# A padded scratch tile moves TensorE's moving operands by 32 bytes in SBUF

## The chip, the cores and the metric

The kernel runs on one core of one Trainium2 chip. The metric is the device time of one execution in microseconds (us); lower is better. The core has five engines that matter here: TensorE (PE in the profile, its weight loads PEld), VectorE (DVE), ScalarE (ACT), GpSimd (POOL) and SyncE (SP, which issues DMAs). SBUF is the on-chip memory of 128 partitions in which every tile lies; PSUM takes TensorE's results.

## The reference

The input is `x` of 8 batches, 3072 positions and 256 features. It goes through a two-dimensional Fourier transform of which the real part is kept, and each of the 24576 rows then goes through a small network with one hidden layer of 2048.

```python
X = np.fft.fft(np.fft.fft(x, axis=1), axis=2).real      # 8 x 3072 x 256
h = X.reshape(-1, 256) @ w_in                            # 24576 x 2048
g = h * np.tanh(np.log1p(np.exp(h)))                     # Mish
out = g @ w_out                                          # 24576 x 256
```

All of it is float32, and the kernel keeps float32 accuracy in matrix products by splitting each factor into a high and a low part.

## The kernel before

The feature transform is multiplied into `w_in` once at the start, which gives a cosine weight and a sine weight. Each is split in two tiles, `wch` and `wcl`, `wsh` and `wsl`; the output weights are `woh` and `wol`. The position transform uses symmetry: DVE and POOL fold the rows of a batch into the tiles `F0e`, `F0o`, `F1e` and `F1o`, and TensorE multiplies these, as weights, with a table `dft`, as the moving operand (`transform`, L365, plain float32). A matmul here has two operands: the weights are loaded into the array beforehand by a LDWEIGHTS (128 columns), and the moving operand is streamed through column by column.

The results of `transform` are combined and split by `first_chunk`, `other_chunks` and `last_chunk` into the tiles `ph`, `pl`, `qh` and `ql`. A batch has three chunks of 512 columns, a chunk 16 steps of the main loop, and the loop 8 x 3 x 16 = 384 steps. The tile `base` is a scratch tile of these functions: DVE writes a result of `transform` there, and the scaling and splitting instructions read it.

Each step of the main loop does this:

- `mm1` (L695 to L697): six matmuls of 512 columns, moving `ph`, `pl`, `qh`, `ql` (type float32r), weights a slice of `wch`, `wcl`, `wsh`, `wsl`.
- `make_h` (L704 to L706): DVE takes the two PSUM results into a ring of nine tiles, `hring`; ACT then applies Mish (L810).
- `split`, eight steps later: ACT casts to `gh` (L714), POOL subtracts to `gl` (L715).
- `mm2`, ten steps later: twelve matmuls of 512 columns (L725), moving `gh` (eight) and `gl` (four), weights slices of `woh` and `wol`.

So a step has 18 such matmuls, each with its own LDWEIGHTS, and the order on each engine is written out by hand. Between steps stand the fold of the next batch, the `transform` matmuls, and once, in the last batch, `single_h` and `single_out`, which compute one position left out by the symmetry. In `single_out` (L783 to L785) the roles are turned round: `woh` and `wol` are moving, 256 columns at a time, and the weights are 8 columns of `endgh` or `endgl`, which lie in the places of `F1e` and `F1o`.

Where a tile lies is set by the order of the pools. The built program puts each tile at the next multiple of 32 bytes in the partition, in the order constants, fold tiles (`fold`, where `base` stands after the `F` tiles and ahead of `full0`, `full1` and `spare`), the split tiles (`ql`, `pl`, `ph`, `qh`), `p0b`, `ot`, and the tiles `gl` and `gh`. In bytes past a multiple of 64, the built program has:

| tile | role in the matmuls | before |
|---|---|---|
| wch, wcl, wsh, wsl, woh, wol | weights in the main loop; woh and wol move in `single_out` | 32 |
| ph, pl, qh, ql, gh, gl | moving, float32r, 512 columns | 0 |
| F0e, F0o, F1e, F1o | weights of `transform` | 32 |
| dft (slices) | moving, float32: 0, 8, 16 or 24 for the even outputs, 16 (`F0`) and 32 (`F1`) for the odd ones | 0 to 32 |
| hring, xring | read and written by DVE, ACT and POOL | 0 |

Past a multiple of 512 all six moving tiles lie at 0, and all slices of the main loop's weights at 288.

Of the kernel before, what the change touches and what calls it, by code (L numbers as in the profile page):

```python
# [10 lines left out]
F32 = mybir.dt.float32  # L11
# [18 lines left out]
NE = 258  # L30
# [182 lines left out]
def fft_moe(ctx, tc, x, col_d, mids_d, w_in, w_out, cs_d, dft_d, ysel_d, out, single_d):  # L213
# [4 lines left out]
    def pool(name, bufs=1, **kw):  # L218
        return ctx.enter_context(tc.tile_pool(name=name, bufs=bufs, **kw))
# [3 lines left out]
    fp = pool("fold")  # L223
# [7 lines left out]
    def ps(tag):  # L231
        return psab.tile([128, 512], F32, tag=tag, name=tag)
# [48 lines left out]
    def fold_part(b, c, y, i, par):  # L281
        return folds[b][c, y][:, par if COSINE[y][i] else 1 - par, i]
# [71 lines left out]
    def const(c, par, sine):  # L354
        if par == 0:
            o = NE * sine
            return dft[:, c, o:o + NE]
        o = 2 * NE + 256 * sine
        return dft[:, c, o:o + 256]

    def transform(dst, lhs, par, sine, mid_lhs=None, halves=(0, 1), **kw):

        last = 1 if mid_lhs is None else 2
        for c in halves:
            T.matmul(dst, lhs(c), const(c, par, sine), **{"start": c == 0, "stop": c == last, **kw})  # L365
        if mid_lhs is not None and 1 in halves:

            n = dst.shape[-1]
            T.matmul(dst, mid_lhs, alt[0:1, None, :].to_broadcast([1, n // 2, 2]), **{**kw, "start": False, "stop": True})
# [3 lines left out]
    def new_chunk(ch):  # L373
        q = {}
        for n in ("ph", "pl", "qh", "ql"):
            q[n] = pqp.tile([128, 512], F32R, tag=n, name=n)
        chunks[ch] = q

    def split_to(hi, lo, src, eng):
        A.copy(hi, src)  # L380
        eng.tensor_tensor(lo, src, hi, op=ALU.subtract)  # L381

    def add_mid(dst, src, i, b):

        pairs = (y[:, :NE].rearrange("p (a s) -> p a s", s=2) for y in (dst, src))
        dst, src = pairs
        V.scalar_tensor_tensor(dst, alt[:, None, :].to_broadcast([128, NE // 2, 2]), midc[:, i, b:b + 1], src,
                               op0=ALU.mult, op1=ALU.add)

    def first_chunk(b, par, part=(0, 1, 2)):  # L390

        ch = 3 * b
        st = folds[b]
        n = NE if par == 0 else 256
        sl = slice(256 * par, 256 * par + 256)
        if 0 in part:
            st["ps", par] = ps("pa"), ps("pb")
        pa, pb = st["ps", par]
        halves = [c for c in (0, 1) if c in part]
        transform(pa[:, :n], lambda c: fold_part(b, c, "e", 0, par), par, 0, None, halves)  # L400
        transform(pb[:, :n], lambda c: fold_part(b, c, "o", 0, par), par, 1, None, halves)
        if b == 0 and par == 1 and 1 in part:

            T.matmul(pb[:, :n], mid0, const(0, 1, 1)[0:1], start=False, stop=True, skip_group_check=True)
        if 2 in part:
            if par == 0:
                new_chunk(ch)
            q = chunks[ch]
            if par == 0:
                base = fp.tile([128, NE], F32, tag="base", name="base")  # L410
                add_mid(base, pa, 0, b)
                pa = base
            split_to(q["ph"][:, sl], q["pl"][:, sl], pa[:, :256], V)
            split_to(q["qh"][:, sl], q["ql"][:, sl], pb[:, :256], V)
            if par == 0:
                V.tensor_copy(ends[:, b:b + 1], pa[:, 256:257])

    def other_chunks(b, par, odd):

        ch = 3 * b + 1  # L420
        if par == 0 and not odd:
            new_chunk(ch)
            for o in range(2):
                full2[o] = fp.tile([128, 512], F32, tag=f"full{o}", name=f"full{o}")
        st = folds[b]
        n = NE if par == 0 else 256
        sl = slice(256 * par, 256 * par + 256)
        pa, pb = ps("pa"), ps("pb")
        y, cos, sin = ("o", 2, 1) if odd else ("e", 1, 2)
        transform(pa[:, :n], lambda c: fold_part(b, c, y, cos, par), par, 0)  # L430
        transform(pb[:, :n], lambda c: fold_part(b, c, y, sin, par), par, 1)

        base = fp.tile([128, NE], F32, tag="base", name="base")
        spare = fp.tile([128, 256], F32, tag="spare", name="spare")
        if par == 0:
            add_mid(base, pa, 1 + odd, b)
        else:
            V.tensor_copy(base[:, :n], pa[:, :n])

        def combine(dst, sg, o):  # L440
            scaled, plain = (base, pb) if odd else (pb, base)
            V.scalar_tensor_tensor(dst, scaled[:, o:o + 256], sg, plain[:, o:o + 256], op0=ALU.mult, op1=ALU.add)

        combine(spare, R3 if odd else -R3, 0)
        q = chunks[ch]
        h, l = ("qh", "ql") if odd else ("ph", "pl")
        split_to(q[h][:, sl], q[l][:, sl], spare, G)
        combine(full2[odd][:, sl], -R3 if odd else R3, 1 if par == 0 else 0)
# [225 lines left out]
    def chunk0(par, part):  # L674
        first_chunk(0, par, (part,))
# [115 lines left out]
    for tau in range(NS + LAG_M):  # L791
# [17 lines left out]
        if tau < NS:  # L809
            A.activation(hring[:, tau % RH], hring[:, tau % RH], AF.Mish)  # L810
            for f in early.pop(tau, []):
                f()
            other_at = OTHER_AT if b else OTHER0_AT
            if r in other_at:
                i = other_at.index(r)
                other_chunks(b, i % 2, i // 2)
            if r in LAST_AT:
                last_chunk(b, LAST_AT.index(r))
            if r == FOLD_AT[b > 0] and b + 1 < NB:
                fold_q = fold_ops(b + 1)  # L820
                pace = sum(cost for cost, _ in fold_q) / (FOLD_AT[2] - r)
                spent = goal = 0.0
            if fold_q:
                goal += pace
                while fold_q and spent + fold_q[0][0] / 2 <= goal + 1e-9 or fold_q and r == FOLD_AT[2]:
                    cost, f = fold_q.pop(0)
                    spent += cost
                    f()
            if b + 1 < NB and r in FIRST_AT:
                first_chunk(b + 1, FIRST_AT.index(r))  # L830
            if tau % NF == P0_AT and tau // NF + 1 < 3 * NB:
                load_p0(tau // NF + 1)
            if b == NB - 1 and r == 20:
                single = single_h()
            if b == NB - 1 and r == 22:
                single_out(single)
# [29 lines left out]
```

## Time and profile before

| | |
|---|---|
| median of 3 runs | 1838.26 us (1837.71 to 1840.17) |
| the profiled execution | 1837.48 us, of which the trace spans 1835.7 us |
| TensorE matmuls (PE) busy | 1773.7 us, 97% of the span |
| TensorE weight loads (PEld) busy | 1410.2 us, 77% |
| DVE, ACT, POOL busy | 1229.0, 903.7, 1236.4 us (67%, 49%, 67%) |
| mean granted TensorE clock | 0.982 of full |

Busy time of matmuls overlaps with that of the next ones, since matmuls are pipelined: one of 512 columns is shown as some 0.40 us long, while the next starts before that time is up. What a matmul costs in a chain of them is read from the distance between starts. The granted clock is given as a share of 2.4 GHz, so 0.50 is 1.2 GHz.

### The profile page before, as it was taken

How to read it: one execution, taken by the hardware profiler on the slowest of the kernel's cores; microseconds unless marked ns; L12 is line 12 of the kernel's file. 1: busy time of each engine (PE TensorE's matmuls, PEld its weight loads, DVE VectorE, ACT ScalarE, POOL GpSimd, SP SyncE). 2: the span in 40 equal slices, each digit the busy share in tenths (PEclk: the TensorE clock that was granted, in tenths of full speed). 3: DMA queues.
4: the chain of work that ended last, by engine and by line, in shares of the span. 5: the costliest groups of instructions: out<-in, count | busy, mean ns of one | idle time of the engine just before them, and what ended most of it. 6: DMA issues, size and time to landing. Idle time of an engine off the chain costs nothing.

```text
span 1835.7 us, 20673 instructions
## 1 busy us (share of the span) xinstructions
PE 1773.7 (97%) x7540; PEld 1410.2 (77%) x7540; DVE 1229.0 (67%) x1609; ACT 903.7 (49%) x980; POOL 1236.4 (67%) x653
## 2 busy tenths in 40 slices
PE   5688999999999999999999999999999999998999
PEld 3366778888888888888888888888888888887887
DVE  7566785677856876577856777568865778553552
ACT  2455454455545555455545555455544555452453
POOL 4368885687756876587756876578765877553556
PEclk8789999999999999999999999999999999998999
DMA  4120200200002000100002000020002000000000
GB/s 170 35 76 29 80 26 4 98 1 30 29 1 98 29 1 29 60 39 29 29 1 98 28 3 29 1 98 29 12 18 97 1 29 30 1 29 1 30 24 23
DMA packets 25016, 67.65 MB, mean 37 GB/s; under 512 B 3027, under 2 KB 3258, under 8 KB 24786
## 3 DMA queue, kind: packets, MB, share of 16 engines
q1 hardware_dynamic: 24354, 64.86, 9.6%
q8 instruction: 59, 0.97, 0.2%
q10 hardware_dynamic: 560, 1.47, 0.2%
q14 instruction: 43, 0.35, 0.1%
HBM read 41.07 MB, written 25.25 MB: 36 GB/s over the span
## 4 chain that ended last, share of the span: by engine, by line
PE 90%; POOL 4%; DVE 2%; issue 2%; ACT 1%; DMA 1%; SPq 0%; DVEq 0%; POOLq 0%
PE acc L725 56%; PE pa L695 5%; PE pa L696 5%; PE pb L695 5%; PE pa L697 5%; PE pb L697 5%; PE pb L696 5%; PE pa L365 2%; PE pb L365 2%; POOL gl L715 1%; ACT gh L714 1%; PE pw L518 1%; POOL xring L504 1%; POOL xring L505 0%; DVE hring L704 0%
## 5 line engine op out<-in xcount | busy, mean ns | idle before, releaser
L715 POOL TENSOR_TENSOR gl<-hring,gh 128x1024 fp32r<-128x1024 f32 x384 | 925.6, 2411 | 515.8 <-ACT gh L714 477.2
L714 ACT CAST gh<-hring 128x1024 fp32r<-128x1024 f32 x384 | 402.8, 1049 | 464.4 <-PE acc L725 464.1
L725 PE MATMUL acc<-gh,woh 128*128 128x512 f32 x1536 | 609.0, 396 | 4.0 <-ACT gh L714 2.2
L725 PE MATMUL acc<-gh,wol 128*128 128x512 f32 x1536 | 607.4, 395 | 0.0
L810 ACT ACTIVATE hring<-hring 128x1024 f32<-128x1024 f32 x384 | 407.3, 1061 | 338.1 <-DVE hring L706 312.9
L704 DVE SCALAR_TENSOR_TENSOR hring<-p0b,wc,pa 128x512 f32<-128x512 f32 x384 | 285.3, 743 | 425.6 <-POOL gl L715 411.8
L725 PE MATMUL acc<-gl,woh 128*128 128x512 f32 x1536 | 433.7, 396 | 2.2 <-POOL gl L715 2.2
L725 PEld LDWEIGHTS acc<-gh,woh 128*128 128x128 f32 x1536 | 288.6, 188 | 76.6 <-ACT gh L714 3.5
L725 PEld LDWEIGHTS acc<-gl,woh 128*128 128x128 f32 x1536 | 288.7, 188 | 73.3 <-POOL gl L715 3.5
L725 PEld LDWEIGHTS acc<-gh,wol 128*128 128x128 f32 x1536 | 289.0, 188 | 69.4 <-POOL wol L537 0.4
L705 DVE TENSOR_TENSOR hring<-hring,pb 128x512 f32<-128x512 f32 x384 | 264.1, 688 | 41.1 <-PE acc L725 0.9
L706 DVE TENSOR_TENSOR hring<-hring,pb 128x512 f32<-128x512 f32 x384 | 263.7, 687 | 13.3
L695 PE MATMUL pa<-ph,wch 128*128 128x512 f32 x384 | 162.8, 424 | 4.0 <-DVE hring L704 4.0
L695 PE MATMUL pb<-qh,wsh 128*128 128x512 f32 x384 | 153.4, 399 | 3.0 <-DVE hring L706 2.6
L696 PE MATMUL pb<-ql,wsh 128*128 128x512 f32 x384 | 152.5, 397 | 0.3 <-POOL ql L381 0.3
L697 PE MATMUL pa<-ph,wcl 128*128 128x512 f32 x384 | 152.6, 398 | 0.0
L696 PE MATMUL pa<-pl,wch 128*128 128x512 f32 x384 | 152.6, 397 | 0.0
L697 PE MATMUL pb<-qh,wsl 128*128 128x512 f32 x384 | 152.3, 396 | 0.0
L695 PEld LDWEIGHTS pb<-qh,wsh 128*128 128x128 f32 x384 | 72.9, 190 | 23.8 <-DVE hring L706 6.0
L695 PEld LDWEIGHTS pa<-ph,wch 128*128 128x128 f32 x384 | 72.6, 189 | 23.3 <-DVE hring L704 4.9
L696 PEld LDWEIGHTS pb<-ql,wsh 128*128 128x128 f32 x384 | 72.6, 189 | 18.0 <-POOL ql L381 0.6
L697 PEld LDWEIGHTS pa<-ph,wcl 128*128 128x128 f32 x384 | 72.6, 189 | 17.7
(192 smaller groups left out, 1343.3 us busy)
## 6 DMA issues: line engine op xcount, KB each, us to landing
xring<-x_dram SPq DMA_DIRECT2D x32, 768.0 KB
out_dram<-ot SPq DMA_DIRECT2D x96, 256.0 KB
p0b<-p_d SPq DMA_DIRECT2D x23, 256.0 KB
xring<-w_out_dram SPq DMA_DIRECT2D x8, 512.0 KB
hring<-w_in_dram SPq DMA_DIRECT2D x4, 512.0 KB
dft<-table_dft_dram ACTq DMA_DIRECT2D x1, 1028.0 KB
winr<-w_in_dram SPq DMA_DIRECT2D x2, 512.0 KB
xring<-w_in_dram SPq DMA_DIRECT2D x2, 512.0 KB
```

What stands on the lines that cost most here:

```text
L365: T.matmul(dst, lhs(c), const(c, par, sine), **{"start": c == 0, "stop": c == last, **kw})
L504: G.tensor_tensor(t, t, vf, op=ALU.add)
L695: T.matmul(dst, wh[:, fs], q[n + "h"], start=True, stop=False)
L696: T.matmul(dst, wh[:, fs], q[n + "l"], start=False, stop=False)
L697: T.matmul(dst, wl[:, fs], q[n + "h"], start=False, stop=True)
L704: V.scalar_tensor_tensor(h[:, 0:512], p0b[ch], wc0[:, f:f + 1], pa, op0=ALU.mult, op1=ALU.add)
L705: V.tensor_tensor(h[:, 512:1024], h[:, 0:512], pb, op=ALU.add)
L706: V.tensor_tensor(h[:, 0:512], h[:, 0:512], pb, op=ALU.subtract)
L714: A.copy(gh, h)
L715: G.tensor_tensor(gl, h, gh, op=ALU.subtract)
L725: T.matmul(acc[i], w[:, f, 128 * d:128 * d + 128], g[:, 512 * t:512 * t + 512], **kw)
L810: A.activation(hring[:, tau % RH], hring[:, tau % RH], AF.Mish)
```

## The change

The scratch tile `base` is allocated 14 float32 longer, 1088 bytes in a partition and not 1032, and is used through a view of its first 258 columns as before. The padding is never read or written.

```diff
             if par == 0:
-                base = fp.tile([128, NE], F32, tag="base", name="base")
+                base = fp.tile([128, NE + 14], F32, tag="base", name="base")[:, :NE]
                 add_mid(base, pa, 0, b)
...
-        base = fp.tile([128, NE], F32, tag="base", name="base")
+        base = fp.tile([128, NE + 14], F32, tag="base", name="base")[:, :NE]
         spare = fp.tile([128, 256], F32, tag="spare", name="spare")
```

No engine's instructions change in number, order or waits. In the built programs the room taken by `base` grows from 1056 to 1088 bytes, and each tile behind it lies 32 bytes further: `full0`, `full1`, `spare`, `ph`, `pl`, `qh`, `ql`, `p0b`, `ot`, `gh`, `gl` go from 0 to 32 past a multiple of 64 (and of 512). All others stay where they were: the weights, `dft`, the `F` tiles, `hring`, `xring`, and `base` itself.

## Rows read from the trace of the kernel before

**Rows 1.** The page: span and busy time of each engine.
```profile
span 1835.7 us, 20673 instructions
PE 1773.7 (97%) x7540; PEld 1410.2 (77%) x7540; DVE 1229.0 (67%) x1609; ACT 903.7 (49%) x980; POOL 1236.4 (67%) x653
```
**Rows 2.** Stretches of the main part: busy us and instructions, clock, DMA share, GB/s.
```profile
core 0: us, PE busy (x) PEld busy (x) DVE busy (x) ACT busy (x) POOL busy (x), PEclk, DMA share, GB/s
500.00:1000.00 500.00, 500.00 (x2155) 404.79 (x2155) 343.18 (x440) 252.90 (x265) 341.18 (x173) 1.00 0.10 38
1000.00:1500.00 500.00, 500.00 (x2152) 404.17 (x2151) 358.36 (x445) 256.34 (x265) 357.16 (x184) 1.00 0.09 32
```
**Rows 3.** Waits, longest in total: us, times, longest.
```profile
POOL gl L715 <- ACT gh L714: 477.2, 271, 16.7
ACT gh L714 <- PE acc L725: 464.1, 357, 11.5
DVE hring L704 <- POOL gl L715: 411.8, 214, 5.0
ACT hring L810 <- DVE hring L706: 312.9, 304, 3.1
```
**Rows 4.** The page: costliest groups of matmuls, with counts.
```profile
L725 PE MATMUL acc<-gh,woh 128*128 128x512 f32 x1536 | 609.0, 396 | 4.0 <-ACT gh L714 2.2
L725 PE MATMUL acc<-gh,wol 128*128 128x512 f32 x1536 | 607.4, 395 | 0.0
...
L725 PE MATMUL acc<-gl,woh 128*128 128x512 f32 x1536 | 433.7, 396 | 2.2 <-POOL gl L715 2.2
...
L695 PE MATMUL pa<-ph,wch 128*128 128x512 f32 x384 | 162.8, 424 | 4.0 <-DVE hring L704 4.0
```
**Rows 5.** Timeline of PE over one step, first and last rows: start us, us.
```profile
800.60 0.40 PE L695 MATMUL pa<-ph,wch 128*128 128x512 f32 x1
800.84 0.40 PE L696 MATMUL pa<-pl,wch 128*128 128x512 f32 x1
...
803.87 1.10 PE L725 MATMUL acc<-gl,woh 128*128 128x512 f32 x4
804.80 0.40 PE L695 MATMUL pa<-ph,wch 128*128 128x512 f32 x1
```
**Rows 6.** Timeline of PE, `transform` of the odd outputs.
```profile
500.29 0.59 PE L365 MATMUL pa<-dft,F0e 128*128 128x256 f32 x2
500.72 0.59 PE L365 MATMUL pa<-dft,F1e 128*128 128x256 f32 x2
501.15 0.59 PE L365 MATMUL pb<-dft,F0o 128*128 128x256 f32 x2
501.58 0.59 PE L365 MATMUL pb<-dft,F1o 128*128 128x256 f32 x2
```
**Rows 7.** Timeline of PE in a stretch of lower clock.
```profile
206.04 0.63 PE L695 MATMUL pa<-ph,wch 128*128 128x512 f32 x1
206.47 0.63 PE L696 MATMUL pa<-pl,wch 128*128 128x512 f32 x1
206.89 0.63 PE L697 MATMUL pa<-ph,wcl 128*128 128x512 f32 x1
```
**Rows 8.** Windows: clock in that stretch and at the end of `single_out`.
```profile
204.20:207.40 3.20, 3.20 (x9) 2.45 (x9) 3.06 (x5) 1.62 (x2) 3.04 (x2) 0.50 0.65 206
...
1697.00:1698.30 1.30, 1.30 (x14) 1.02 (x12) 0.00 (x0) 0.00 (x0) 0.00 (x0) 1.00 0.07 13
```
**Rows 9.** Timeline of PE, last matmuls of `single_out`.
```profile
1697.08 0.28 PE L783 MATMUL pa<-woh,endgh 128*8 128x256 f32 x1
1697.19 0.28 PE L784 MATMUL pa<-wol,endgh 128*8 128x256 f32 x1
...
1698.32 0.28 PE L785 MATMUL pa<-woh,endgl 128*8 128x256 f32 x1
```
**Rows 10.** Weight loads by form: the main loop's, and `single_out`'s: busy us, mean ns.
```profile
L725 PEld LDWEIGHTS acc<-gh,wol 128*128 128x128 f32 x1536 | 289.0, 188 | 69.4 <-POOL wol L537 0.4
...
L365 PEld LDWEIGHTS pb<-dft,F1o 128*128 128x128 f32 x64 | 12.0, 189 | 2.0 <-DVE F1o L319 0.3
...
L784 PEld LDWEIGHTS pa<-wol,endgh 128*8 128x8 f32 x4 | 0.4, 88 | 0.1
```

## The prediction

> **What bounds the kernel now.** I read the page's first part, then the stretches, then the waits. TensorE's matmuls are busy for 1773.7 us of the 1835.7 us span [rows 1], and between 500 and 1500 us without a gap, at a granted clock of 1.00 [rows 2]. The other engines are busy 50 to 72% there, and the waits that they lead, ACT's for TensorE (464.1 us) and through it POOL's and DVE's, end at TensorE's work [rows 3]. So the end of the kernel moves with what one matmul costs from its start to the next one's, and with nothing else as long as POOL and DVE keep their 28 to 32% of slack.
>
> That cost is read from the timeline. A step of the main loop goes from 800.60 to 804.80 us [rows 5] and has 18 matmuls of 512 columns: 4.20 / 18 = 0.2333 us each. There are 3 x 1536 + 6 x 384 = 6912 of them [rows 4], and 6912 x 0.2333 = 1613 us, 88% of the span. One nanosecond on each is 6.9 us, 0.38% of the time.
>
> Now what the 233 ns consist of. The plain float32 matmuls of `transform` start at 500.29 and at 501.58 us with six passes between, 1.29 / 6 = 0.215 us for a pass [rows 6]. Their weight loads are as long as the main loop's, 189 and 188 ns [rows 10]. In the stretch with a granted clock of 0.50 (1.2 GHz) [rows 8], main-loop matmuls start 0.85 / 2 = 0.425 us apart [rows 7], some 213 ns at full speed if the clock were all. So at 2.4 GHz a float32r matmul of 512 columns costs about 18 ns more than the 215 ns of a float32 pass, with the same weight load beside it. At 1.2 GHz the excess is not there. I read it as the moving columns not always coming as fast as the array at 2.4 GHz takes them. It is 18 x 6912 = 124 us in all, and it is the one thing that the place of a moving operand could change.
>
> **The change part by part.** Nothing is added, removed or reordered on any engine. Two kinds of access change place.
>
> First, DVE, ACT and POOL read or write `ph` to `ql`, `full0`, `full1`, `spare`, `p0b`, `ot`, `gh` and `gl` 32 bytes further. I cost this at nothing. The cover is the slack of [rows 2]: POOL, the busiest, has 341 of 500 us filled and would have to become some 45% slower before TensorE waits for it. What gains there buys nothing either, since these engines wait for TensorE [rows 3]. With the cover gone, 1% on POOL would cost some 12 us. The DMAs that write `p0b` and read `ot` move with them, and DMA is busy 10% of that time.
>
> Second, the moving operand of all 6912 matmuls goes from 0 to 32 past a multiple of 64, while the weights stay at 32. This is the whole sum: 6912 x (new start-to-start time - 233.3 ns). The trace has no matmul of this form with a moving operand at 32. The nearest row is `single_out`: there `woh` and `wol`, at 32 past a multiple of 64, are streamed as float32r at full clock [rows 8]. From 1697.08 to 1698.32 us stand eleven starts, 1.24 / 11 = 0.1127 us; with a reading error of 0.01 us on either end, 0.113 us for 256 columns [rows 9]. Twice that is 226 ns for 512 columns, against 233. So moving columns at 32 come at least as fast as those at 0, and perhaps 7 ns in 512 columns faster. But these matmuls differ in a second thing: their weight loads have 8 columns, not 128, and last 88 ns, not 188 [rows 10]. If the 7 ns belong to the weight load that runs beside, the change gains none of them; if they belong to the place, all. No row tells these apart.
>
> The bounds are so: at best the excess goes whole, -18 ns, -124 us; by the row of `single_out` taken full, -7 ns, -48 us; no change, 0. On the losing side the price of a collision with the weight load: 120 columns more make a load 188 - 88 = 100 ns longer [rows 10], 0.83 ns per column. The load's 512 bytes are eight pieces of 64; if each held up the moving stream by one such column time, it would be +6.7 ns, +46 us. I take half of what `single_out` shows, 3.4 ns, because half of the difference between the two rows (place, weight load) is at issue: 6912 x 3.4 ns = 23.5 us less. The profiled execution took 1837.5 us, so 1814; the median of the runs is 0.8 us above it, so **1815 us**.
>
> **The rivals.** *No change.* The 18 ns belong to float32r at full clock wherever it lies, or to the weight load beside it. For it: the passes of `transform` take the same 0.43 us a pair whether `dft` moves from 16 past a multiple of 64 (`F0`) or from 32 (`F1`) [rows 6]. Against it: those take a column at half the rate, at which even the lower clock shows no excess, so they could not show a shortage. It gives 1838 us.
>
> The Trainium skill speaks for this rival twice. "SBUF - State Buffer", Specifications, has lines of 16 bytes as the unit of access, and 32 bytes are two whole lines, so by it nothing should change; no row here shows lines of any length. "TensorE: Matmul & The Clock Gate", Part 2, gives TensorE two independent read ports and says that loading weights takes no bandwidth from the running matmul, and Part 1 that a warm matmul of 512 columns costs 215.7 ns from start to start, which by itself would make the main loop 1491 us. The trace agrees for the float32 passes (0.215 us) and not for the main loop (0.233 us), so the page does not cover what is at issue.
>
> *Slower.* Today the moving stream and the weight load start in different halves of a 64-byte piece; after the change both start in the same half. If two reads of one half hold each other up, the excess of today is the smaller of two, and the change picks the larger. For it: an excess exists, and only where columns are taken at full rate with a load of 128 columns does it reach 18 ns. Against it: the load walks through its 512 bytes while 2048 bytes of columns go by, so the halves meet many times whatever the start, and `single_out` has moving operands at 32 with weight columns at 32 and at 0 in turn (`endgh` is stepped by 32 bytes) with starts that stay 0.11 us apart. Price as above, +46 us: 1884. It decides from +0.5 ns per matmul, which is 3.7 us, 0.2%; that is about what a measurement of this kernel can tell from no change.
>
> *Another engine becomes the bound.* With POOL's casts slower by 45% it would pass TensorE. Under 3%, and it counts with slower.
>
> *The shift does not arrive.* The places were read in the two built programs, so I give it nothing.
>
> **How the numbers follow.** A small effect per matmul is enough to be seen, which keeps "no change" from being the most likely although no row speaks against it. Faster 0.40, because the only full-rate row with a moving operand at 32 is the faster one; no change 0.32; slower 0.28, for the shared half. Within "faster" I expect 1768 to 1834 us, from an effect of 10 ns down to one of 0.5 ns. Over all cases 1770 to 1883 us: below it lies the part of "faster" in which more than half of the excess goes (0.08), above it a collision dearer than one column time for each piece (0.12).
>
> **What would show it.** In the changed kernel a step between two L695 matmuls on `pa` at full clock would be 4.14 us, not 4.20; 4.08 if `single_out`'s rate holds in full, 4.20 for no change, 4.32 for the collision. `transform`, `single_out` and stretches at 1.2 GHz, where a matmul takes 0.427 us, should stay as they are. The mean durations of L714, L715 and L704 to L706 should not move by over 5%, and POOL and DVE should not begin to end TensorE's waits. The prediction is wrong if the step is 4.20 us to within 0.01, or longer, or if the step shrinks while the time goes to waits of TensorE.

## The result, and the profile after

The changed kernel takes 1796.91 us (median, 1796.19 to 1798.39), against 1838.41 us before: a ratio of 0.9774 with a 95% interval of 0.9757 to 0.9791. The forecast was 1815 us, faster; the gain is 41.5 us where 23.5 were forecast.

The page of the changed kernel, span and busy times of the engines, and the costliest groups (idle time and releaser behind the second bar):

```profile
span 1795.4 us, 20673 instructions
PE 1734.0 (97%) x7540; PEld 1409.8 (79%) x7540; DVE 1210.5 (67%) x1609; ACT 900.8 (50%) x980; POOL 1236.6 (69%) x653
...
L715 POOL TENSOR_TENSOR gl<-hring,gh 128x1024 fp32r<-128x1024 f32 x384 | 926.7, 2414 | 473.8 <-ACT gh L714 325.7
L725 PE MATMUL acc<-gh,woh 128*128 128x512 f32 x1536 | 599.2, 390 | 4.4 <-ACT gh L714 2.5
...
L714 ACT CAST gh<-hring 128x1024 fp32r<-128x1024 f32 x384 | 403.2, 1050 | 380.5 <-PE acc L725 379.8
```

Beside [rows 1, 4]: the same instructions, 40 us less span, and 39.7 us less matmul time. The weight loads take what they took (1409.8 against 1410.2 us). TensorE waits hardly longer than before: 4.4 us ahead of the first group, where it was 4.0. ACT still waits for TensorE most (379.8 us, 464.1 before [rows 3]); these engines do the same work in less time and are idle less.

The timeline of PE over one step of the changed kernel, to be held against [rows 5]:

```profile
802.87 0.39 PE L695 MATMUL pa<-ph,wch 128*128 128x512 f32 x1
803.09 0.39 PE L696 MATMUL pa<-pl,wch 128*128 128x512 f32 x1
...
806.04 1.07 PE L725 MATMUL acc<-gl,woh 128*128 128x512 f32 x4
806.95 0.39 PE L695 MATMUL pa<-ph,wch 128*128 128x512 f32 x1
```

806.95 - 802.87 = 4.08 us for 18 matmuls, 226.7 ns each, where it was 4.20 and 233.3. From here on a step is read over ten steps, from the summary by line: count of matmuls; shortest, median and longest duration in ns; first and last start in the stretch. A quiet step is one with its 18 matmuls and nothing else on TensorE, no wait in it, at full clock. For the kernel before and the changed one:

```profile
L695 PE MATMUL pa<-ph,wch x11: 396/396/396, 800.6 to 842.6; 128*128 128x512 f32 x11
```
```profile
L695 PE MATMUL pa<-ph,wch x11: 389/389/389, 802.9 to 843.7; 128*128 128x512 f32 x11
```

42.0 us against 40.8 us for ten steps. 6.67 ns less on 6912 matmuls would be 46.1 us; the span fell by 40.3. The same summary over the first and the second batch (48 steps each) tells where the rest is; first before the change, then after:

```profile
L695 PE MATMUL pa<-ph,wch x49: 395/396/1415, 41.5 to 298.5; 128*128 128x512 f32 x49
...
L695 PE MATMUL pa<-ph,wch x49: 396/396/586, 298.5 to 510.4; 128*128 128x512 f32 x49
```
```profile
L695 PE MATMUL pa<-ph,wch x49: 387/389/1415, 41.3 to 297.4; 128*128 128x512 f32 x49
...
L695 PE MATMUL pa<-ph,wch x49: 389/389/585, 297.4 to 503.8; 128*128 128x512 f32 x49
```

The second batch goes from 211.9 to 206.4 us, 5.5 us, near the 5.8 that 48 x 0.12 gives. The first goes from 257.0 to 256.1. About twenty of its 48 steps are quiet and gain 0.12 us each, but others wait for weights that are still being converted, or hold other matmuls, and these take as long as before or longer: TensorE is idle for 32.1 us of the first batch before the change and for 32.6 after it.

### The profile page after: what moved, and what is told of

It reads as the page before. It is cut to its first block, busy times and chain, and to the rows that moved or that the text cites. A ratio compares the mean times of both kernels' runs of the same rounds, so it can differ in the third digit from the quotient of the medians.

```text
span 1795.4 us, 20673 instructions
## 1 busy us (share of the span) xinstructions
PE 1734.0 (97%) x7540; PEld 1409.8 (79%) x7540; DVE 1210.5 (67%) x1609; ACT 900.8 (50%) x980; POOL 1236.6 (69%) x653
## 4 chain that ended last, share of the span: by engine, by line
PE 88%; POOL 5%; DVE 2%; issue 2%; ACT 2%; DMA 1%; SPq 0%; DVEq 0%; POOLq 0%
PE acc L725 55%; PE pa L695 5%; PE pa L696 5%; PE pa L697 5%; PE pb L695 4%; PE pb L696 4%; PE pb L697 4%; POOL gl L715 2%; PE pa L365 2%; PE pb L365 2%; ACT gh L714 1%; POOL xring L504 1%; POOL xring L505 1%; PE pw L518 1%; DVE hring L704 1%
## 5 line engine op out<-in xcount | busy, mean ns | idle before, releaser
L715 POOL TENSOR_TENSOR gl<-hring,gh 128x1024 fp32r<-128x1024 f32 x384 | 926.7, 2414 | 473.8 <-ACT gh L714 325.7
L725 PE MATMUL acc<-gh,woh 128*128 128x512 f32 x1536 | 599.2, 390 | 4.4 <-ACT gh L714 2.5
L725 PE MATMUL acc<-gh,wol 128*128 128x512 f32 x1536 | 598.4, 390 | 0.0
L714 ACT CAST gh<-hring 128x1024 fp32r<-128x1024 f32 x384 | 403.2, 1050 | 380.5 <-PE acc L725 379.8
L725 PE MATMUL acc<-gl,woh 128*128 128x512 f32 x1536 | 423.6, 390 | 2.4 <-POOL gl L715 2.3
```

Of the source, the lines that this page charges most:

```text
L714: A.copy(gh, h)
L715: G.tensor_tensor(gl, h, gh, op=ALU.subtract)
L725: T.matmul(acc[i], w[:, f, 128 * d:128 * d + 128], g[:, 512 * t:512 * t + 512], **kw)
```

## The experiments

Twelve kernels ran. All starts below are in bytes past a multiple of 256 or 512 in the partition, as the built programs have them.

**Which operand's place counts.** Theory A: the moving operand's own. Theory B: that moving operands and weights start alike. In the kernel before the small tile `alt` lies ahead of the weights; making it longer pushes the weights and all behind them by 32 bytes. The first run does that to the changed kernel, the second to the kernel before.

```diff
-    alt = cp.tile([128, 2], F32, name="alt")
+    alt = cp.tile([128, 16], F32, name="alt")[:, :2]
```

First run (weights at 320, moving at 64 past a multiple of 512):

> Weights and moving operands both lie at 0 past a multiple of 64 (in the changed kernel both lie at 32); their distance is the same as in the changed kernel. Theory A, the moving operand's own place decides: moving at 0 is the slow place, so a step of 4.20 us and a time of 1838 us, as before the change. Theory B, what counts is that both operands start in the same half of 64 bytes: a step of 4.08 us and 1797 us, as after the change.

1798.37 us, ratio 0.9777 (0.9762 to 0.9791), and ten steps in 40.9 us:

```profile
L695 PE MATMUL pa<-ph,wch x11: 389/389/398, 800.9 to 841.8; 128*128 128x512 f32 x11
```

Second run (weights at 320, moving at 32):

> The weights move to 0 past a multiple of 64 and the moving operands to 32, so the distance between them is that of the kernel before. Theory A (place of the moving operand): a step of 4.08 us and 1797 us; and single_out, whose moving operands are the weights tiles and so now lie at 0, slows from 113.3 to 116.7 ns per matmul of 256 columns. Theory B (same half): a step of 4.20 us and 1838 us, single_out as before.

1839.56 us, ratio 0.9999 (0.9990 to 1.0009), ten steps in 42.0 us:

```profile
L695 PE MATMUL pa<-ph,wch x11: 395/395/395, 803.3 to 845.3; 128*128 128x512 f32 x11
```

Theory A falls on both sides: moving operands at 0 past a multiple of 64 are fast here, and at 32, where the changed kernel has them, they are slow. B gives both numbers. The second run settles another point as well: `p0b`, `ot`, `full0`, `full1` and `spare` lie there where the changed kernel has them, and nothing is gained, so none of the gain comes from the other engines' operands. The second sign of the expectation, `single_out`, told nothing: its operands lie at the same places in both runs, yet of its last starts at full clock ten take 1.17 us in the first run and 1.13 in the second.

**One part of the tiles, and a first sweep.** Each of the six tiles was made 64 bytes longer and used through a view that starts a given number of columns in (`PLACE` holds length and start in columns):

```diff
-            q[n] = pqp.tile([128, 512], F32R, tag=n, name=n)
+            w, o = PLACE[n]
+            q[n] = pqp.tile([128, 512 + w], F32R, tag=n, name=n)[:, o:o + 512]
...
-        gh = gp.tile([128, 1024], F32R, tag="gh", name="gh")
+        gh = gp.tile([128, 1024 + PLACE["gh"][0]], F32R, tag="gh", name="gh")[:, PLACE["gh"][1]:PLACE["gh"][1] + 1024]
```

> Only gh and gl, the moving operands of the twelve second-layer matmuls of a step, go to 32; ph, pl, qh and ql stay at 0, as do p0b, ot, full0, full1 and spare. If the gain is TensorE's alone and adds up matmul by matmul: twelve at 226.7 and six at 233.3 ns, a step of 4.12 us, and two thirds of the gain, about 28 us: 1811 us. If the places of the other engines' tiles bring part of it, the step stays above 4.12 us.

1832.51 us, ratio 0.9967 (0.9956 to 0.9978): 6 us, not 28. A step over ten is 4.18 us, not 4.12:

```profile
L699 PE MATMUL pa<-ph,wch x11: 393/395/397, 803.4 to 845.2; 128*128 128x512 f32 x11
```

The miss has a reason that I had not seen when writing the expectation. Tiles lengthened by 64 bytes put the second buffer of each pair, and the tiles behind, at other places: `gl` at 32 and 96 and `gh` at 160 and 224 past a multiple of 512, and the eight first-layer buffers at 0, 64, ... 448. All of `gl` and `gh` are 32 past a multiple of 64. So "the same half of 64 bytes" can't be the whole of B.

> Each of the six moving tiles lies at another distance past a multiple of 64: qh 8, ph 16, ql 24, gl 40, pl 48, gh 56 bytes; weights at 32. Read from the start-to-start times by tile. Theory A with a step at the half (32-byte pieces): 8, 16 and 24 cost 233 ns, 40, 48 and 56 cost 227. Theory A with a penalty for anything off 32: all six cost 233 or more. Theory B: by the shared half the same as the first, so this run tells only whether the effect is a step, a ramp or a single good place.

One execution, 1829.85 us. It mixes places in the same way (buffers at 0 to 448 plus the offset), and the start-to-start times spread from 225 to 256 ns, and those of one tile, `qh`, from 231 to 256, so it tells nothing by tile. What it showed is that a matmul's time is not set by its own tile alone, and that a map needs all tiles at one place for a while.

**The map.** All buffers of `ph`, `pl`, `qh`, `ql` were put in one long tile, those of `gh` and `gl` in another, buffers a multiple of 512 bytes apart, and the start is shifted per batch (`SH`, in columns). To make room the third pair of `w_in` tiles is converted in `xring`, and two scratch tiles of the start (`cs`, `mids`) go to `full1` and `full0`. In the two kernels of 64-byte steps these loads overwrite part of the first batch's input, so its outputs are wrong.

```diff
-            q[n] = pqp.tile([128, 512], F32R, tag=n, name=n)
+            i = {"ql": (ch + 1) % 2, "pl": 2 + (ch + 1) % 2, "ph": 4 + ch % 2, "qh": 6 + ch % 2}[n]; q[n] = big[:, SH[ch // 3] + 512 * i:SH[ch // 3] + 512 * i + 512]
...
-        gh = gp.tile([128, 1024], F32R, tag="gh", name="gh")
-        gl = gp.tile([128, 1024], F32R, tag="gl", name="gl")
+        o = SH[s // (3 * NF)] + 1024 * (s % 2); gh = gbig[:, o:o + 1024]
+        gl = gbig[:, 2048 + o:2048 + o + 1024]
```

> Weights as in the kernel before (288 past a multiple of 512). The six moving tiles lie in two long tiles and are shifted anew in each batch: batch 0 to 7 at 0, 64, 128, ... 448 bytes past a multiple of 512. Read is the length of a quiet step in each batch. Theory B1, only the half of 64 bytes in which the two operands start counts: 4.20 us in all eight batches. Theory B2, the distance between the two operands within 512 bytes counts, and two operands start well or badly apart: 4.20 in batch 0, and other batches differ from it, some longer and some shorter, which the uneven start-to-start times of the run with gh and gl alone at 32 speak for.

> As the run before it, but batch 0 to 7 at 32, 96, 160, ... 480 bytes past a multiple of 512. Theory B1: 4.08 us in all eight batches. Theory B2: 4.08 in batch 0, other lengths in others, so that the sixteen steps of the two runs make a smooth band over the distance from the weights.

> The long moving tiles again, batch 0 to 7 at +4, +8, +12, +16, +20, +24, -8 and -16 bytes from the good place (where the distance to the weights is a multiple of 256). Theory C1, a step at 32 bytes: the six positive ones 4.08 us, the two negative ones 4.15 to 4.20. Theory C2, a single good place: all eight longer than 4.08. Theory C3, the places of lowest cost lie between and 4.08 is not the floor: some below 4.08. If 0.1133 us per 256 columns, which single_out showed with loads of 8 columns, is the rate of a float32r stream that no load disturbs, nothing falls below 4.08.

> The map over 256 bytes filled in: each of the 24 chunks has all its moving tiles at another place, multiples of 8 bytes not measured so far (8, 72, 80, 88, 104, ... 248), with 0, 32 and 36 again as controls (4.20, 4.08, 4.27). Theory F, 0.1133 us per 256 columns is the floor of a float32r stream: nothing below 4.08. Rival: another place lies below 4.08, so that a faster kernel than the changed one can be had by its tiles' places alone.

In the last of the four the start changes per chunk; at each change some columns of a neighbouring buffer are overwritten before their last use, so some outputs there are wrong, and TensorE waits at the changes, which is why its total (1962.85 us) means nothing. The other totals are mixtures too (1850.63, 1833.95 and 1847.22 us). What counts is the quiet step. Of the run with places 32, 96, ... 480, the rows of batches 0, 1, 2 and 4, ten steps each:

```profile
L695 PE MATMUL pa<-big,wch x11: 389/389/389, 219.5 to 260.3; 128*128 128x512 f32 x11
...
L695 PE MATMUL pa<-big,wch x11: 388/388/388, 429.2 to 470.4; 128*128 128x512 f32 x11
...
L695 PE MATMUL pa<-big,wch x11: 390/392/404, 641.0 to 682.9; 128*128 128x512 f32 x11
...
L695 PE MATMUL pa<-big,wch x11: 389/389/389, 1065.5 to 1106.3; 128*128 128x512 f32 x11
```

40.8, 41.2, 41.9 and 40.8 us: place 32 and place 288 agree, and so do all pairs 256 apart, here (96 and 352, 160 and 416, 224 and 480) and in the run with 0, 64, ... 448 (0.2 ns per matmul at most). So the distance of moving operand and weights counts within 256 bytes. Two of the run around the good place, +12 and +20 bytes from it:

```profile
L695 PE MATMUL pa<-big,wch x11: 391/391/391, 641.5 to 682.7; 128*128 128x512 f32 x11
...
L695 PE MATMUL pa<-big,wch x11: 404/404/404, 1067.8 to 1111.0; 128*128 128x512 f32 x11
```

41.2 and 43.2 us. The whole map, distance (moving minus weights, within 256 bytes) and length of a quiet step in us, from the four traces. The multiples of 8 that only the last of the four has rest on two to five quiet steps each, the others on ten or more.

| distance | step | distance | step | distance | step |
|---|---|---|---|---|---|
| 0 | 4.08 | 72 | 4.23 | 168 | 4.19 |
| 4 | 4.25 to 4.27 | 80 | 4.16 | 176 | 4.20 |
| 8 | 4.20 | 88 | 4.19 | 184 | 4.17 |
| 12 | 4.12 | 96, 104 | 4.20 | 192 | 4.20 |
| 16 | 4.17 | 112 | 4.16 | 200 | 4.18 |
| 20 | 4.32 | 120 | 4.23 | 208, 232 | 4.22 |
| 24 | 4.21 | 128 | 4.18 | 216 | 4.21 |
| 32, 40, 48 | 4.20 | 136, 144, 152 | 4.20 | 224 | 4.20 |
| 56 | 4.17 | 160 | 4.22 | 240 | 4.20, later 4.26 |
| 64 | 4.12 | | | 248 | 4.18 and 4.21 |

Theory B1 (halves of 64 bytes) falls, B2 holds, but not as a smooth band: one place at 4.08, two at 4.12, most near 4.20, and the worst only 20 bytes from the best. The kernel before stood at distance 224, the changed one at 0. C1 and C3 fall, C2 stands; F holds on every place measured: none is below 4.08. These are 35 of the 64 distances that are multiples of 4, so no measured place beats the changed kernel's, and the others are open.

At a few distances the map has two lengths, because the main loop held two rates there at one and the same place. At distance 240 its batch ran at 4.20 us a step before `single_out` came and at 4.26 after it, both at full clock:

```profile
L695 PE MATMUL pa<-big,wch x11: 394/394/394, 1626.5 to 1668.5; 128*128 128x512 f32 x11
...
L695 PE MATMUL pa<-big,wch x11: 402/402/403, 1736.0 to 1778.6; 128*128 128x512 f32 x11
```

At 248 the steps go from 4.18 to 4.21 and back within a batch. At 0 and 224, the two distances that the change is about, the quiet steps of all runs agree.

**Does each matmul pay for itself?** The same long tiles, with the first layer's and the second layer's shifted apart; as before, columns at the changes of place are overwritten, so some outputs there are wrong. A place of 32 is distance 0, a place of 0 is distance 224.

> Weights as in the kernel before. The first layer's moving tiles (ph, pl, qh, ql) and the second layer's (gh, gl) are placed apart, batch by batch, in bytes past a multiple of 256, first layer / second layer: 0/0, 32/0, 0/32, 32/32, 32/160, 160/32, and then 32/32 twice with one of them a further 256 away. If each matmul pays for its own place: 4.20, 4.16, 4.12, 4.08, then 32/160 and 160/32 between (160 alone gave 4.185 over all 18: some 4.15 and 4.115), and 4.08 twice. If it is the string of matmuls that settles into a rhythm: the mixed batches lie elsewhere, and 32/0 or 0/32 may gain nothing.

Batches 1, 2, 3 and 6 (32/0, 0/32, 32/32, 32/288), ten steps each:

```profile
L695 PE MATMUL pa<-big,wch x11: 392/392/393, 433.2 to 475.0; 128*128 128x512 f32 x11
...
L695 PE MATMUL pa<-big,wch x11: 397/397/397, 646.3 to 687.8; 128*128 128x512 f32 x11
...
L695 PE MATMUL pa<-big,wch x11: 389/389/389, 854.2 to 895.0; 128*128 128x512 f32 x11
...
L695 PE MATMUL pa<-big,wch x11: 389/389/389, 1484.5 to 1525.3; 128*128 128x512 f32 x11
```

4.187 and 4.147 us from the starts, where paying alone would give 4.16 and 4.12, and 4.08 for the last two. Both mixed batches are 0.027 us over. (32/160 and 160/32 came to 4.167 and 4.127, where the separate sums are 4.15 and 4.115, so 17 and 12 ns over.) So a step is near the sum of what its matmuls cost at their own distances, with 12 to 27 ns on top. The timeline tells where the 27 ns are: the first starts of each layer in batch 2 (second layer at distance 0), with the seventh of its twelve:

```profile
646.35 0.40 PE L695 MATMUL pa<-big,wch 128*128 128x512 f32 x1
...
647.75 0.39 PE L725 MATMUL acc<-gbig,woh 128*128 128x512 f32 x1
...
649.13 0.39 PE L725 MATMUL acc<-gbig,woh 128*128 128x512 f32 x1
...
650.49 0.40 PE L695 MATMUL pa<-big,wch 128*128 128x512 f32 x1
```

The six at distance 224 take 1.40 us, 233.3 ns each. The first six at distance 0 take 1.38 (the trace has 230, 236, 228, 232, 231 and 227 ns), and the last six 1.36, 226.7 each. In batch 1, where only six matmuls stand at distance 0, they take the same 1.38 us and never come down to 226.7 on the mean. So in these two batches the cost of the changes lies in the six matmuls after the string has come to the good distance.

That shifting the late tiles alone gave 6 us has mostly another reason: `gh` stood at distances 128 and 192 and `gl` half the time at 64. By the map the places of all tiles of that run add up to some 4.175 us (an estimate), against 4.18 measured.

**Is it the length of the load, and whose?** In the kernel before and then in the changed one, second-layer loads are cut to 8 columns (and the copies and stores of the results to the 8 rows that are then computed):

```diff
-            T.matmul(acc[i], w[:, f, 128 * d:128 * d + 128], g[:, 512 * t:512 * t + 512], **kw)
+            T.matmul(acc[i][:8], w[:, f, 128 * d:128 * d + 8], g[:, 512 * t:512 * t + 512], **kw)
```

> All places as in the kernel before; the second layer's weight loads take 8 columns and not 128, so only 8 of each 128 output features are computed and stored. Theory L, the time lost is the load of the next weights meeting the moving stream in SBUF: the twelve second-layer matmuls and the last first-layer one have short loads beside them, eleven of the twelve by the load of the next second-layer one, so 12 at 226.7 and 6 at 233.3 ns, a step of 4.12 us. Rival, the excess is the moving stream's own at that place: 4.20 us.

> The changed kernel with second-layer weight loads of 8 columns and not 128 (8 of each 128 output features are computed and stored). The same cut in the kernel before gave 4.18 us, not the 4.12 that the length of the load would have given. If the start of the load against the stream is what counts, not its length, the good place stays good: 4.08 us. If the cut itself adds a cost of its own, the step is longer than 4.08; if the length of the load still costs something at the good place, it is shorter.

Ten steps of the first, and of the second:

```profile
L695 PE MATMUL pa<-ph,wch x11: 395/396/397, 642.5 to 684.3; 128*128 128x512 f32 x11
```
```profile
L695 PE MATMUL pa<-ph,wch x11: 389/389/389, 632.4 to 673.2; 128*128 128x512 f32 x11
```

4.18 and 4.08 us (totals 1830.70 and 1795.62). Theory L falls in its simple form: a load of a sixteenth of the columns, which lasts 88 to 90 ns and not 188, saves 20 ns in a step of 4.20, not 80, and at the good place it saves nothing at all. The first of these runs also holds a surprise. Its `single_out` is untouched and every operand of it lies where it lay before the change, yet its matmuls of 256 columns start 0.117 us apart at full clock, where [rows 9] have 0.113:

```profile
1691.64 0.28 PE L784 MATMUL pa<-wol,endgh 128*8 128x256 f32 x1
...
1692.81 0.28 PE L785 MATMUL pa<-woh,endgl 128*8 128x256 f32 x1
```

1.17 us for ten. The same string at the same places can thus run at either of two rates, 0.1133 and 0.1167, half of 226.7 and of 233.3. In the run that shifted the late tiles alone, one string of `single_out` shows both, one after the other, at full clock:

```profile
1689.80 0.28 PE L789 MATMUL pa<-woh,endgl 128*8 128x256 f32 x1
...
1690.97 0.28 PE L787 MATMUL pa<-woh,endgh 128*8 128x256 f32 x1
...
1691.78 0.28 PE L788 MATMUL pa<-wol,endgh 128*8 128x256 f32 x1
...
1692.91 0.28 PE L789 MATMUL pa<-woh,endgl 128*8 128x256 f32 x1
```

1.17 us for ten starts, and then 1.13 for ten.

Last, the changed kernel with one weights tile, `wol`, 32 bytes off (`woh` 32 bytes longer, `base` of its old length):

```diff
-    woh = cp.tile([128, NF, D], F32R, name="woh")
+    woh = cp.tile([128, NF * D + 8], F32R, name="woh")[:, :NF * D].rearrange("p (f d) -> p f d", f=NF)
```

> As the changed kernel (all moving tiles 0 past a multiple of 256 from the weights), but one weights tile, wol, lies 32 bytes further. In the string gh/woh, gh/wol, gh/woh, ... each matmul has the load of the next one's weights beside it. Theory N, it is the load beside that counts: gh/woh, with wol's load beside, costs some 233 ns, gh/wol 227. Theory O, a matmul's own weights count: the other way round. Theory P, only the moving place decides: 227 for all and a step of 4.08 us. By N and O, with about 13 ns for each change of distance within the string, the step is some 4.19 to 4.21 us.

One execution, 1825.98 us, a step of 4.16 us, so P falls. It is also less than the 4.19 to 4.21 that N and O gave: four matmuls at 233.3 ns would make 4.107, so the eight changes of distance in a step cost under 7 ns each here, and the 13 ns of the expectation are no fixed price. The timeline of PE from the clean first-layer matmuls into the second layer:

```profile
803.29 0.39 PE L696 MATMUL pb<-ql,wsh 128*128 128x512 f32 x1
803.52 0.39 PE L697 MATMUL pb<-qh,wsl 128*128 128x512 f32 x1
803.74 0.40 PE L725 MATMUL acc<-gh,woh 128*128 128x512 f32 x1
803.98 0.39 PE L725 MATMUL acc<-gh,wol 128*128 128x512 f32 x1
804.21 0.40 PE L725 MATMUL acc<-gh,woh 128*128 128x512 f32 x1
```

803.52 to 803.74 is 0.226 us in the trace, the good rate; the first `gh`/`woh`, which has `wol`'s load beside it and no `wol` matmul before it, already takes 0.235. That is for N. Further in, `gh`/`wol` is the longer of the two (236 to 240 against 231 to 233 ns), which N does not give, and the four `gl`/`woh` and two first-layer matmuls after them, with no `wol` in them, still swing between 224 and 236. So here the disturbance begins with the load beside and lives on for several matmuls; N and O are not told apart beyond its first.

## Why the prediction was right, and where not

**The bound.** Right. TensorE's start-to-start time set the end before and after; no other engine's durations moved (L715 2411 to 2414 ns, L714 1049 to 1050), and POOL, at 369 of 500 us in its busiest stretch, did not begin to limit. Two readings beside it were a little off: in [rows 2] DVE is as full as POOL (343 and 358 us), and by the fuller stretch the room is 40%, not 45%.

**The excess as the thing at stake.** Right, and bounded: at the lower clock main-loop matmuls of the changed kernel start 0.427 us apart as before (205.29 to 207.85 us, six of them, granted clock 0.50), and at full clock, of the 18 ns above a float32 pass 6.7 could be had by place; some 12 (226.7 against 215) stayed at every place of the map, and no run here shows what they are.

**The term of the sum.** The sign was right and the term was mis-sized: "I take half of what `single_out` shows, 3.4 ns" measured 6.67, the whole of what `single_out` showed. Half was the mean of two outcomes, all or nothing, and as the prediction argued it the time could only come out as one of the two. The other factor was a little too large: 6912 matmuls, of which the first batch's 864 gained 0.9 us and not 5.8, since TensorE waits for other work there. (Two bounds beside the sum are off by a little: 0.5 ns per matmul is 3.5 us, not 3.7, and half of the excess ends at 1776 us, not at 1770.)

**The reason behind the term.** This step failed, although its number was near: "moving columns at 32 come at least as fast as those at 0" took the place of the moving operand for the cause. The two runs that move the weights show that the distance to the weights is the cause, with the moving operand at 32 slow and at 0 fast. And `single_out` was no measure of a place: at the same places it ran at 0.117 in another kernel. Its 0.1133 is a rate that a string of float32r matmuls can hold, and the main loop reaches it at one distance. So the direction came out right by luck: the 32 bytes happened to take the distance from 224 to 0, the one place of 35 that gives 4.08 us, and had the padding moved the weights along, nothing would have been gained.

**The rivals.** *No change* fell, with its pointer, the float32 passes, which indeed don't show the effect (0.43 us a pair after as before). The Trainium skill's "SBUF — State Buffer", Specifications, gives lines of 16 bytes, and as the prediction read it a shift of two whole lines should not have mattered; the runs disagree: 32 bytes were worth 6.7 ns, and distances 16, 32 and 48 bytes from the good one gave 4.17, 4.20 and 4.20 us. The Trainium skill's "TensorE: Matmul & The Clock Gate", Part 2, says that loading weights takes no bandwidth from the running matmul. The runs agree as far as the load's length costs nothing at the good distance (4.08 us with 128 columns and with 8); they do not let one ignore the weights, since where these lie against the stream costs up to 13 ns per matmul (4.32 us), and a load moved by 32 bytes went with 235 ns, not 227, for the matmul beside it. *Slower* named the right pair, the places of TensorE's two operands against each other, and had its sign turned: starting alike is the good case. That the two reads hold each other up, as it argued, is not shown. *Another engine* and *the shift does not arrive* did not happen.

**What stays open.** Why one distance in 256 bytes is good and one 20 bytes on is the worst, and why a string can run at two rates at the same places. What the runs show (regular rates, six matmuls to settle after a change of distance, a disturbance that outlives its cause, one string that goes from 117 to 113 ns) is what a string of matmuls and loads that falls into a repeating rhythm would show. That the rhythm is the cause is an argument, not a measurement, and no run here looked below one matmul.

## What to carry to other kernels

Where TensorE is the bound with float32r operands, read the start-to-start time of a quiet string at full clock against that of a float32 pass; if it stands above 0.2267 us for 512 columns, look at the places of both operands in the partition before anything else. Try moving operands and weights a multiple of 256 bytes apart, the best of the places measured here, and all of them, since a mixture loses more than its share (12 to 53 ns a step here); recheck after every change of a tile's size ahead of them. A row that differs in two things from the case at hand bounds a cost but does not name its cause: moving the other operand is the cheap test.

## What the runs showed of the hardware that was not expected

The time of a float32r matmul of 512 columns at full clock, with a load of 128 columns beside it, depends on the distance between its moving operand and the weights modulo 256 bytes, from 226.7 ns (distance 0) to 240.0 ns (distance 20). It is no smooth band: 16, 20 and 24 bytes give 4.17, 4.32 and 4.21 us a step. It was the distance and not the place that counted, as far as one common shift of 32 bytes tells (1798.37 against 1796.91 us, ratios 0.9777 and 0.9774). A string that changes distance twice in 18 matmuls pays 12 to 27 ns on top, and where it was looked at, in the six matmuls after the change to the good distance. And one string at the same places can hold two rates: `single_out`, 256 columns with loads of 8, ran at 113.3 ns in the kernel before and the changed one and at 116.7 in a kernel with the same places, and the main loop at distance 240 at 4.20 and 4.26 us.
